# FFN by 26 block products in place of 28, on tiles of 1024 tokens, with the sums of weights kept in DRAM

## The chip, the cores and the metric

One core of a Trainium2 chip. The metric is the device time of one execution in microseconds. The kernel before takes 1181.1 us (median of 3 runs, 1180.2 to 1182.3). A ratio is the one for the fast runs of the same rounds, with its 95% interval; it is not quite the ratio of the medians that stand next to it. A kernel counts as faster or slower when it differs by 2%. Starts of parts are read from the one profiled run of each kernel.

## The reference

Eight batches of eight heads, 576 positions, 64 features a head; the result of the attention is reordered into 4608 tokens of 512 features and goes through a gated feed-forward network (FFN).

```python
def _attn_ref(q, k, v):                       # q, k, v: (8, 8, 576, 64)
    scores = scale * np.matmul(q, k.transpose(0, 1, 3, 2))
    ...                                       # Dmat: gamma ** (row - column), 0 above the diagonal
    return np.matmul(scores * Dmat, v)

def _moe_ref(x, w_gate, w_val, w_out):        # x: (4608, 512), d_ff = 1536
    g = x @ w_gate
    silu = g * (1.0 / (1.0 + np.exp(-g)))
    return silu * (x @ w_val) @ w_out
```

## The kernel before

The kernel first does four attention steps and a plain FFN tile of 512 tokens, while VectorE and ScalarE round the weights from 64-bit floats. All later tiles (512 tokens each) use seven block products in place of eight; the sums of blocks that they need are made on GpSimd and VectorE during the tile. Attention steps are merged between the products of the tile before the one that needs them. In the first stage a weight block goes through this ring: load of raw bits, split on ScalarE, rounding on VectorE; a finished split starts a load three blocks on.

```python
    def split(i):
        ...
        nc.scalar.activation(out=top, in_=bits[:, :, 1].bitcast(F32), func=AF.Copy, scale=2.0 ** -112)
        nc.scalar.activation(out=ulp, in_=bits[:, :, 0].bitcast(U32), func=AF.Copy, scale=2.0 ** -29)
        if order.index(i) + RAWS < len(order):
            load_w(order[order.index(i) + RAWS])      # on SyncE's queue

    def weight(i):                                    # VectorE, three operations
        nc.vector.tensor_scalar(out=dst, in0=top, scalar1=3, ...)
        nc.vector.scalar_tensor_tensor(out=top, in0=top, ..., in1=dst, ...)
        nc.vector.tensor_tensor(out=dst, in0=top, in1=ulp, op=ALU.add)
        ...                                           # then split() of the next block
```

The schedule is manual: the program fixes the order of each engine's instructions.

## Time and profile before

| part of the kernel before | us | read from |
|---|---|---|
| first stage: attention and plain tile of 512 tokens | 207.0 | start of the first block product |
| eight tiles of 7 products, with the remaining attention | 973.6 | 1180.6 less 207.0 |
| TensorE's share of the span | 97% | first line of the page |

The prediction shows the lines that carry this.

### The profile page before, as it was taken

To read this page: it belongs to the slowest core of one execution; us is meant where nothing else is said; L and a number is where in the kernel's file an instruction comes from. 1 tells how busy PE (TensorE), PEld (TensorE's weight loads), DVE (VectorE), ACT (ScalarE), POOL (GpSimd) and SP (SyncE) were. 2 spreads that over 40 slices of the span, in tenths; PEclk is the share of its full clock that TensorE was granted. 3 is DMA by queue.
4 is the path that set the end of the run, shared out by engine and by line. 5 is a ranking of instruction groups with operands and counts; after the bars stand their busy time and mean duration, and the time that the engine had idled before them with its cause. 6 is when DMAs were issued, how large, how long until landed. Compare 5 with 4: busy or idle time off the path is not lost.

```text
span 1180.6 us, 16347 instructions
## 1 busy us (share of the span) xinstructions
PE 1150.1 (97%) x6660; PEld 944.7 (80%) x6660; DVE 484.2 (41%) x886; ACT 186.8 (16%) x342; POOL 425.1 (36%) x384
## 2 busy tenths in 40 slices
PE   6988899999999999999999999999999999999998
PEld 5534444888888888888888888888888888888887
DVE  3566642444444433544244444444443333333332
ACT  3443310111011101111011101110111011101110
POOL 1000010443345343344444414434453435345641
PEclk9988899999999999999999999999999999999999
DMA  7897422222213221222222222222000010000001
GB/s 189 243 259 194 120 49 57 49 39 41 55 34 65 41 39 37 39 53 45 58 40 41 39 66 49 40 40 48 28 1 1 1 36 1 1 18 19 1 1 36
DMA packets 228300, 65.33 MB, mean 55 GB/s; under 512 B 211712, under 2 KB 219904, under 8 KB 228224
## 3 DMA queue, kind: packets, MB, share of 16 engines
q1 hardware_dynamic: 228224, 64.27, 23.5%
q8 instruction: 53, 0.87, 0.3%
q14 instruction: 23, 0.19, 0.1%
HBM read 54.80 MB, written 9.44 MB: 54 GB/s over the span
## 4 chain that ended last, share of the span: by engine, by line
PE 92%; SPq 4%; DVE 1%; DMA 1%; ACT 1%; issue 0%; DVEq 0%; ACTq 0%
PE bankE L394 14%; PE bankA L394 14%; PE bankC L394 14%; PE bankE L464 7%; PE bankC L464 7%; PE bankB L394 7%; PE bankA L464 7%; PE bankB L464 4%; PE sc L277 2%; PE xo L299 2%; PE mix L283 2%; PE bankA L351 2%; SPq L132 2%; PE xo L307 1%; PE bankC L351 1%; PE bankE L351 1%
## 5 line engine op out<-in xcount | busy, mean ns | idle before, releaser
L394 PE MATMUL bankA<-x,w_up 128*128 128x256 f32 x768 | 182.0, 380 | 0.0
L438 POOL TENSOR_TENSOR hid<-c,ss 128x512 f32<-128x512 f32 x48 | 61.0, 1271 | 325.2 <-ACT ss L437 325.2
L394 PEld LDWEIGHTS bankA<-x,w_up 128*128 128x128 f32 x768 | 145.4, 190 | 20.4 <-issue 0.5
L413 DVE TENSOR_TENSOR u<-bankB,u 128x512 f32<-128x512 f32 x48 | 33.2, 692 | 147.7 <-PE bankB L394 138.2
L394 PE MATMUL bankE<-x,s 128*128 128x256 f32 x384 | 91.3, 381 | 0.0
L394 PE MATMUL bankE<-x,w_up 128*128 128x256 f32 x384 | 91.3, 381 | 0.0
L394 PE MATMUL bankC<-t,s 128*128 128x256 f32 x384 | 90.7, 379 | 0.0
L394 PE MATMUL bankC<-t,w_up 128*128 128x256 f32 x384 | 90.7, 379 | 0.0
L394 PE MATMUL bankB<-t,s 128*128 128x256 f32 x384 | 90.7, 379 | 0.0
L464 PE MATMUL bankE<-w_dn,hid 128*128 128x256 f32 x384 | 86.1, 381 | 0.0
L464 PE MATMUL bankA<-w_dn,hid 128*128 128x256 f32 x384 | 85.5, 379 | 0.0
L464 PE MATMUL bankC<-t,hid 128*128 128x256 f32 x384 | 85.5, 379 | 0.0
L394 PEld LDWEIGHTS bankC<-t,s 128*128 128x128 f32 x384 | 73.0, 190 | 9.9
L394 PEld LDWEIGHTS bankB<-t,s 128*128 128x128 f32 x384 | 73.0, 190 | 9.9
L394 PEld LDWEIGHTS bankC<-t,w_up 128*128 128x128 f32 x384 | 73.0, 190 | 9.9
L464 PEld LDWEIGHTS bankA<-w_dn,hid 128*128 128x128 f32 x384 | 73.0, 190 | 9.9
L464 PEld LDWEIGHTS bankC<-t,hid 128*128 128x128 f32 x384 | 73.0, 190 | 9.9
L394 PEld LDWEIGHTS bankE<-x,w_up 128*128 128x128 f32 x384 | 72.5, 190 | 10.0
L394 PEld LDWEIGHTS bankE<-x,s 128*128 128x128 f32 x384 | 72.5, 190 | 10.0
L464 PEld LDWEIGHTS bankE<-w_dn,hid 128*128 128x128 f32 x384 | 72.5, 190 | 10.0
L429 ACT ACTIVATE s<-bankA 128x256 f32<-128x256 f32 x48 | 18.4, 383 | 345.1 <-PE bankA L394 345.1
L371 POOL TENSOR_TENSOR s<-w_up 128x512 f32<-128x512 f32 x48 | 61.0, 1271 | 7.6 <-DVE w_dn L225 7.6
(107 smaller groups left out, 1520.1 us busy)
## 6 DMA issues: line engine op xcount, KB each, us to landing
kn<-in_k_dram SPq DMA_DIRECT2D x64, 128.0 KB, 2.8
v<-in_v_dram SPq DMA_DIRECT2D x64, 128.0 KB, 2.9
qk<-in_q_dram SPq DMA_DIRECT2D x112, 72.0 KB, 2.5
qk<-in_k_dram SPq DMA_DIRECT2D x112, 72.0 KB, 2.6
raw<-in_moe_w_gate_dram SPq DMA_DIRECT2D x6, 1024.0 KB, 5.4
raw<-in_moe_w_val_dram SPq DMA_DIRECT2D x6, 1024.0 KB, 7.2
raw<-in_moe_w_out_dram SPq DMA_DIRECT2D x6, 1024.0 KB, 5.1
out_dram<-c SPq DMA_DIRECT2D x16, 256.0 KB, 2.2
```

The source lines that it names most:

```text
L132: nc.sync.dma_start(out=qk[a * SQ : (a + 1) * SQ, n], in_=src[b, 2 * p + a // 2, :, (a % 2) * SQ : (a % 2 + 1) * SQ].rearrange("(j t) d -> ...
L277: nc.tensor.matmul(sc[hl][:, ts(c, P)], kT[half[hl], ts(c, P)], qT[half[hl], ts(c, P)], start=True, stop=True)
L283: nc.tensor.matmul(z[half[hl], c], kn[:, c, hl, :], s["v"][:, c, hl, :], start=True, stop=True)
L299: nc.tensor.matmul(xo[half[hl], ts(c, P)], s["v"][:, c, hl, :], ret[:, hl, ts(c, P)], start=(c == 0), stop=(c == 0), skip_group_check=True)
L307: nc.tensor.matmul(o[half[hl]], state[half[hl], c - 1, :], s["qT"][half[hl], c * P : c * P + w], start=False, stop=True, skip_group_check= ...
L351: nc.tensor.matmul(bank, w_up[:, u, gv, c // 2, c % 2, fb, :], x[:, c, :], start=(c == 0), stop=(c == HP - 1))
L371: nc.gpsimd.tensor_tensor(out=s2, in0=A(u, 1, 0), in1=A(u, 0, 0), op=ALU.subtract)
L394: nc.tensor.matmul(bank[:, gv * TH : (gv + 1) * TH], lhs(gv, c), rhs[:, c, :], start=(start and gv == 0 and c == 0), stop=(stop and c == 1 ...
L413: nc.vector.tensor_tensor(out=uu, in0=bankB, in1=uu, op=ALU.add)
L429: nc.scalar.activation(out=s, in_=bankA[:, 0:TH], func=AF.Silu)
L438: nc.gpsimd.tensor_tensor(out=hid[:, u, 1::2], in0=t["c"][:, :, 1], in1=s, op=ALU.mult)
L464: nc.tensor.matmul(bank[:, m * DH : (m + 1) * DH], lhs(u)[:, ts(m, P)], rhs(u), start=(start and u == 0 and m == 0), stop=(stop and u == N ...
```

## The change

The 4x2 by 2x4 block scheme computes with 26 products what takes 32 plain ones, and 28 by the seven for eight of the kernel before. Four tiles of 1024 tokens replace eight of 512, and 144 matmul calls of 256 columns go. To pay for this:

- the 26 operands of gate and value weights (most of them sums of blocks) for each of three groups of four feature blocks, one group a pass, are made once, during the first big tile (1024 tokens), used in place, stored to DRAM, and fetched per tile from then on; the sums of output weights are made by GpSimd in the first stage and stored as well;
- rounding works on halves, and the plain tile's plan says by a table how many halves must be rounded before each block of 128 features;
- memory of finished stages is handed on (x of one tile lies where the raw weights were), and four more attention steps come into the first stage.

The diff, cut to its core (the tables of the products are left out but for two lines):

```diff
-    TW = 512
+    T0 = 512
+    TW = 1024
+UP = [
+    "0= | 8: sub 8 2 6, sub 9 0 8, sub 10 4 9 | 8: neg 8 6, sub 9 2 6, ... | copy 0, copy 1",
+    "1= | 10: sub 11 3 8, sub 12 7 11 | 3: add 12 3 6, neg 12 12 | copy 2, copy 3",
...
+    def up_step(n, qd, i):
+        bank, opens, xslot, xops, wslot, wops, ops = up[i]
+        busy = n == 1
+        if qd == 0 and i > 0:
+            for op in xops:
+                add(nc.vector if busy else nc.gpsimd, op, x_view(n))
+        if busy:
+            if i > 0:
+                for op in wops:
+                    add(nc.gpsimd, op, up_view(qd))
+            w = up_view(qd)(wslot)
+        else:
+            w = operand()[:, 0:512]...                 # from the ring of eight fetched places
...                                                    # 4 matmuls
+        if busy:
+            nc.sync.dma_start(out=up_ops[qd][i]..., in_=w)
+        else:
+            fetch()
...
+    have = {2: 8, 3: 8, 4: 12, 5: 12, 6: 18, 7: 18, 8: 24, 9: 24, 10: 32, 11: 32}
+    for f in range(2, NF):
+        while nxt < have[f]:
+            plan.append(roundings[nxt - done])
+            nxt += 1
+        plan.append(lambda f=f: up0(f, range(HP)))
+        for _ in range(3):
+            if f >= (8, 10, NF)[groups[0][0]]:
+                plan.append(sums_of(groups.pop(0)[1]))   # GpSimd sums, stores on SyncE's queue
...
+    merge((0.5, ticks(HP, 10)), (0.5, plan))
```

## The prediction

> **What bounds the kernel now.** I read the page first (busy shares, chain of waits), then busy time by stretch, the chain in order of time, the groups, the DMA queue's own waits, and the timeline of one attention step.
>
> ```profile
> span 1180.6 us, 16347 instructions
> PE 1150.1 (97%) x6660; PEld 944.7 (80%) x6660; DVE 484.2 (41%) x886; ACT 186.8 (16%) x342; POOL 425.1 (36%) x384
> PE 92%; SPq 4%; DVE 1%; DMA 1%; ACT 1%; issue 0%; DVEq 0%; ACTq 0%
> ```
> TensorE is 97% busy and 92% of the chain. By stretch (span, then busy time of each engine, clock, DMA share, GB/s):
> ```profile
> 78.00:147.00 69.00, 60.64 (x256) 30.30 (x253) 40.05 (x65) 21.81 (x26) 3.83 (x3) 0.86 0.68 185
> 458.50:584.00 125.50, 125.50 (x793) 109.41 (x792) 52.48 (x101) 16.35 (x34) 50.97 (x47) 1.00 0.22 46
> 960.00:1068.00 108.00, 108.00 (x502) 95.08 (x501) 35.52 (x52) 13.25 (x26) 51.32 (x46) 1.00 0.03 10
> ```
> Holes are in the first stage only (here 8 us, clock 0.86). From 207 us on TensorE is full, VectorE and GpSimd near 40%. In the chain in order of time, one product of the up layer is 4 calls (8 records), one of the down layer 12 calls (24 records):
> ```profile
> 78.49 6.15 PE bankA L351 x8
> 84.64 3.43 PE bankB L351 x8
> ...
> 332.85 1.73 PE bankA L394 x8
> ...
> 1042.13 5.18 PE bankB L464 x24
> ```
> So a call of 256 columns costs 1.727/4 = 0.432 us, with no gap between products. The first two lines show the price of a long pause: after 8 us without work, 8 calls took 6.15 us instead of 3.43.
>
> What the other engines pay per operation (busy, mean ns | idle):
> ```profile
> L413 DVE TENSOR_TENSOR u<-bankB,u 128x512 f32<-128x512 f32 x48 | 33.2, 692 | 147.7 <-PE bankB L394 138.2 <-ACT u L408 9.5
> L371 POOL TENSOR_TENSOR s<-w_up 128x512 f32<-128x512 f32 x48 | 61.0, 1271 | 7.6 <-DVE w_dn L225 7.6
> L446 POOL TENSOR_TENSOR hid<-u,s 128x256 f32<-128x256 f32 x48 | 34.9, 727 | 45.1 <-ACT s L445 45.1
> ```
> One attention step in the timeline, from TensorE's first work to its next product, and the loads that follow it on the queue; below it the queue's longest such wait:
> ```profile
> 468.81 1.09 PE L299 MATMUL xo<-ret,v 128*64 128x128 f32 x16
> 472.84 1.99 PE L394 MATMUL bankE<-x,s 128*128 128x256 f32 x8
> 475.17 0.74 DVE L262 STREAM_TRANSPOSE kT<-qk 128x576 f32<-128x576 f32 x1
> 475.94 1.96 SPq L132 DMA_DIRECT2D qk<-in_q_dram  x4
> 482.30 1.15 SPq L142 DMA_DIRECT2D vl<-in_v_dram  x2
> ```
> ```profile
> SPq L132 <- DVE kT L262: 316.7, 21, 20.8
> ```
> Call the step's start T0. TensorE is on it for 4.03 us; VectorE is done at T0+7.1; only then does the queue issue 14 loads at about 0.5 us each, until T0+14.6. Today nothing urgent stands behind them.
>
> [...]
>
> **The change part by part.**
>
> *Removed.* Per 1024 tokens the up layer goes from 2 x 6 x 7 x 4 = 336 calls to 3 x 26 x 4 = 312, the down layer from 2 x 7 x 12 = 168 to 26 x 6 = 156: 36 calls fewer, 15.5 us, and over 4 tiles 62.2 us. The first 512 tokens stay plain. The attention work is the same; four steps of it move from the tiles into the first stage. With TensorE as full as now: 1180.6 - 62.2 = 1118.4.
>
> *VectorE and GpSimd, by amount.* A pass of 26 up products lasts 26 x 1.727 = 44.9 us on TensorE. VectorE has 21 adds from PSUM and 8 products, 21 x 0.69 + 8 x 0.42 = 18 us; GpSimd in the first pass of a later tile 21 sums of x x 1.27 + 4 x 1.27 + 8 x 0.73 = 37.6 us, in the other passes 11. In the first big tile GpSimd makes 30 weight sums a pass[...]. Down: 67 us, against about 32 on VectorE and 23 on GpSimd. All fit by amount; the loss is in order and distance.
>
> *(b) First big tile: a sum's place may be overwritten only when its store to DRAM has landed.* The stores stand on the one queue, behind the loads of an attention step. A store behind them is issued at T0+14.6 and lands 2.3 us later (existing 256 KB stores: 2.2), T0+17.0; the dependent sum and negation end at T0+19. Four steps fall into this tile's up layer, before steps (0,0), (0,19), (1,13), (2,6) of the three passes. At (1,13) the rewritten sum is used at product 18: TensorE is there at T0+4.03+5x1.73 = 12.7, stall 6.4. At (2,6): used at product 10, due T0+10.9, stall 8.1. At (0,0): VectorE starts 1 us late (copies of the plain tile, x sums), used at product 6, due T0+14.4, ready 19.4, stall 5, then 0.8. At (0,19) there is distance; VectorE makes a sum of x late, 2.4. Sum 22.7[...]: 27.
>
> *(c) Later tiles: sums of x on GpSimd, two products ahead of use.* They queue behind GpSimd's part of the step before. Example: product 4 ends at 0; VectorE adds till 0.9, GpSimd subtracts till 2.24, ACT's Silu till 2.7, GpSimd's product till 3.5, then the x sum till 4.8; product 7 was due at 3.46: 1.4 lost. Likewise before products 10 (1.35), 11 (0.9), 19 (1.7; hidden once by an attention step) and 24 (0.8): 6.2, 6.2 and 4.5 us for three tiles. At each of three changes of tile the first x sums wait for GpSimd's last down sums: 1.2 each. Sum 20.5.
>
> *(d) Fetches.* 256 KB per 1.73 us is 152 GB/s. Eight places are a lead of 13.8 us; after an attention step the next fetch lands at about T0+17.7 and is due at T0+17.85. Even, so some 1 us per step for six steps: 6.
>
> *(a) First stage.* The 36 half-size roundings cost VectorE as before, but six attention steps are pressed into the up layer (about 69 us of needed VectorE work against 69 of TensorE before the tenth feature block), and GpSimd's 78 sums of the output weights finish within a few us of the plain tile's end. I take +5; the earlier table load gives little back.
>
> Sum: 1118.4 + 27 + 20.5 + 6 + 5 = 1176.9. I state 1172, a little lower, since each stall was walked separately and a late TensorE gives the next sum more time.
>
> **The rivals.** R1, all hidden: TensorE stays at 99% and the time is about 1120 to 1130. For: before, the same style of schedule runs with no gap; both helpers have over half their time free. Against: distances of two products and a queue that stands for 14.6 us. R2, DMA bound: loads of small packets took 22% of the DMA engines for 46 GB/s; 152 more GB/s at the first stage's rate of about 217 GB/s for 87% busy would add over 60%, so fetches would queue, tiles 2 and 3 by 20 to 40 us: 1195 to 1215. Against: the eight places ahead, and that the weight rows are longer. R3, the first stage waits for the output-weight sums and late roundings: 20 us more, 1190.
>
> **Range and chances.** The gain of 62.2 is sure; (b) and (c) rest on the order of the queues and measured durations and I trust them to about 12 us together; (a) and (d) to 8 each. Root of the squares is near 17 us: 8 in 10 from 1148 to 1196. Faster by over 2% means under 1157.5: 0.25. Slower by over 2% means over 1204.7: 0.05. Within: 0.70.
>
> **What would show each step.** The FFN has 288 TensorE records fewer (two per call, 144 calls); products at 1.73 and 2.59 us. For (b): three TensorE gaps of 5 to 8 us in the first big tile, weight sums on GpSimd waiting for DMA stores, the queue waiting for the transposes. For (c): in the first pass of tiles 2 to 4 TensorE waits of 1 to 2 us released by GpSimd, none in passes two and three. For (d): TensorE waiting for DMA in tiles 2 and 3 only. I am wrong if the first big tile shows no gap (then R1), if tile 4, which has no attention, is much over 202 + 8 us, or if the plain tile ends later than 240 us.

## More of the kernel before

An attention step is three functions that are emitted together. The matmuls of `values` and of `scores` write different columns of one PSUM bank, `mix`, and VectorE empties it in between:

```python
    z, sr, xr = mix[:, 0:256], mix[:, 256:320], mix[:, 384:448]   # shapes shortened
    def tick(t, lo=HP, hi=NP):
        for fn, i in ((values, t - 2), (scores, t - 1), (transposes, t)):
            if lo <= i < hi:
                fn(i)
    # values(i):  TensorE fills xo and xr (bank mix); VectorE: evacuate(xr), evacuate(xo)
    # scores(i):  TensorE fills sc, then sr and z (bank mix); VectorE: ret, ret_last, state
```

One more view is needed for later, busy time by stretch, at the end of the first stage. The columns are the stretch and its length; busy time (and instructions) of TensorE, of its weight loads, of VectorE, ScalarE and GpSimd; granted clock, DMA share, GB/s.

```profile
147.00:207.00 60.00, 60.00 (x265) 29.69 (x264) 19.55 (x38) 6.60 (x11) 6.90 (x6) 1.00 0.24 52
207.00:260.00 53.00, 53.00 (x352) 46.11 (x351) 22.75 (x45) 8.70 (x18) 25.93 (x22) 1.00 0.25 49
```

TensorE has no idle moment in the last 60 us of the first stage. VectorE has 40 us of them free there, and GpSimd 53.

## The result, and the profile after

The changed kernel takes 1247.6 us (median of 4 runs, 1244.4 to 1250.1), against 1181.4 in the same rounds: ratio 1.0559, 95% interval 1.0533 to 1.0586. It is slower by 5.6%, and outside the predicted range.

The first lines of the page, the busy shares and the chain of waits (which the reconstruction loses before it reaches the start):

```profile
span 1245.7 us, 17330 instructions
PE 1112.4 (89%) x6372; PEld 895.8 (72%) x6372; DVE 635.0 (51%) x1031; ACT 247.9 (20%) x508; POOL 489.9 (39%) x422
PE 55%; POOL 5%; DVE 2%; issue 1%; ACT 1%; DVEq 0%; POOLq 0%; ACTq 0%
```

TensorE has exactly 6660 - 6372 = 288 records fewer, as predicted, but its share fell from 97% to 89%. The work went and idle time came. Busy time by stretch says where (columns as above):

```profile
147.00:207.00 60.00, 30.47 (x229) 18.19 (x226) 43.15 (x74) 16.63 (x30) 30.80 (x36) 0.74 0.62 165
260.00:300.00 40.00, 24.53 (x153) 19.81 (x154) 21.36 (x32) 5.56 (x12) 29.40 (x27) 0.86 0.68 190
300.00:350.00 50.00, 41.85 (x225) 34.78 (x225) 38.51 (x54) 9.28 (x21) 33.27 (x23) 0.90 0.43 131
400.00:470.00 70.00, 57.59 (x298) 48.77 (x297) 34.85 (x57) 13.31 (x30) 41.07 (x31) 0.90 0.42 129
470.00:556.00 86.00, 86.00 (x611) 74.35 (x611) 52.06 (x88) 10.74 (x22) 24.06 (x14) 1.00 0.72 198
```

In the stretch 147 to 207 us TensorE worked 30 us of 60, at a clock of 0.74, where it worked all 60 before. The up layer of the first big tile (275 to 476 us) has holes throughout. The down layer (from 476 us) is full.

I cut the program at two moments that the timeline gives, the start of the first block product and the start of the first down product, and set each part beside its nominal length, which is the prediction's base of 1118.4 us: the old first stage and five attention steps of 4.03 us (207.0 + 20.2), three passes of 44.9 us and four attention steps (150.8), and what is left. Five steps, since the first one of the big tile also stands before its first product: the attention's output matmuls ran for 8 steps before that cut in the kernel before, and for 13 now.

| part | nominal | predicted loss | the changed kernel | loss |
|---|---|---|---|---|
| first stage, to the first block product | 227.2 | 5 | 275.1 | 47.9 |
| up layer of the first big tile | 150.8 | 27 | 200.6 | 49.8 |
| the rest | 740.4 | 26.5 | 770.0 | 29.6 |
| sum | 1118.4 | 58.5 | 1245.7 | 127.3 |

What TensorE waited for, in the timeline of TensorE. A line is start, duration, engine, line of the program, operation and operands; in brackets how long the engine was idle before and who released it.

```profile
123.49 0.48 PE L402 MATMUL mix<-qT,kT 64*64 64x64 f32 x4 [7.45 <-DVE x_odd L445]
168.22 0.48 PE L402 MATMUL mix<-qT,kT 64*64 64x64 f32 x4 [19.22 <-DVE x_odd L445]
203.08 0.48 PE L402 MATMUL mix<-qT,kT 64*64 64x64 f32 x4 [9.53 <-DVE rest L445]
275.08 3.78 PE L601 MATMUL bankA<-rest,arena 128*128 128x256 f32 x8 [10.74 <-POOL arena L502]
387.32 3.78 PE L601 MATMUL bankA<-x_odd,arena 128*128 128x256 f32 x8 [7.07 <-POOL arena L502]
437.37 3.78 PE L601 MATMUL bankC<-rest,arena 128*128 128x256 f32 x8 [9.05 <-POOL arena L502]
...
820.23 1.99 PE L601 MATMUL bankA<-rest,arena 128*128 128x256 f32 x8 [1.54 <-POOL rest L504]
826.82 1.99 PE L601 MATMUL bankC<-rest,arena 128*128 128x256 f32 x8 [1.15 <-POOL rest L504]
845.27 1.99 PE L601 MATMUL bankC<-rest,arena 128*128 128x256 f32 x8 [1.61 <-POOL rest L504]
```

Three kinds of wait stand there. In the first stage the scores' matmul into bank `mix` waits for VectorE to empty that bank. In the first big tile a product waits for GpSimd's last weight sum: the waits of 7.07 and 9.05 us are those predicted at 6.4 and 8.1. In the later tiles products wait one microsecond or so for GpSimd's sums of x, as predicted.

Why does VectorE come 19 us late at 168 us? Its own timeline ahead of that moment:

```profile
147.70 0.56 DVE L352 TENSOR_SCALAR rest<-rest 128x512 int32<-128x512 int32 x1
148.30 1.10 DVE L353 SCALAR_TENSOR_TENSOR rest<-rest 128x512 int32<-128x512 int32 x1
149.43 1.09 DVE L355 CUSTOM_DVE_ANT_0 rest<-rest 128x1024 uint16<-128x1024 uint16 x1
...
161.77 0.99 DVE L355 CUSTOM_DVE_ANT_0 arena<-rest 128x1024 uint16<-128x1024 uint16 x1
165.54 0.53 DVE L352 TENSOR_SCALAR arena<-rest 128x512 int32<-128x512 int32 x1 [2.78 <-ACT rest L339]
166.10 1.10 DVE L353 SCALAR_TENSOR_TENSOR rest<-rest,arena 128x512 int32<-128x512 int32 x1
167.34 0.69 DVE L355 CUSTOM_DVE_ANT_0 arena<-rest 128x1024 uint16<-128x1024 uint16 x1
167.95 0.22 DVE L445 TENSOR_TENSOR x_odd<-mix,tab 128x64 f32<-128x64 f32 x1
```

The evacuation that TensorE waits for takes 0.22 us, but it stands in VectorE's queue behind seven half roundings in a row, 20 us of them. The last waits for ScalarE's split, which itself waited 5.5 us for its raw weights. And the two-input operations of the roundings take up to 1.1 us each where they take 0.69 in the run without the sums, below. The table `have` causes the row: it asks for four, six or eight new halves before every second block and for none before the next one.

### The profile page after: what moved, and what is told of

The parts are those of the page before. It is cut to its first block, busy times and chain, and to the rows that moved or that the text cites. A ratio compares the mean times of both kernels' runs of the same rounds, so it can differ in the third digit from the quotient of the medians.

```text
span 1245.7 us, 17330 instructions
## 1 busy us (share of the span) xinstructions
PE 1112.4 (89%) x6372; PEld 895.8 (72%) x6372; DVE 635.0 (51%) x1031; ACT 247.9 (20%) x508; POOL 489.9 (39%) x422
## 4 chain that ended last, share of the span: by engine, by line
PE 55%; POOL 5%; DVE 2%; issue 1%; ACT 1%; DVEq 0%; POOLq 0%; ACTq 0%
PE bankA L601 8%; PE bankE L601 8%; PE bankB L601 7%; PE bankC L601 6%; PE bankC L642 6%; PE bankE L642 6%; PE bankB L642 5%; PE bankA L642 5%; POOL rest L504 3%; DVE rest L580 2%; PE xo L421 1%; PE sc L399 1%; POOL rest L580 1%; POOL arena L622 1%; PE xo L429 1%; PE mix L405 1%
## 5 line engine op out<-in xcount | busy, mean ns | idle before, releaser
L504 POOL TENSOR_TENSOR arena<-arena 128x512 f32<-128x512 f32 (+1 forms) x97 | 152.9, 1592 | 128.4 <-DVE arena L504 58.8
L504 POOL TENSOR_TENSOR rest<-rest 128x256 f32<-128x256 f32 (+1 forms) x111 | 108.6, 990 | 180.1 <-DVE rest L355 110.7
L601 PE MATMUL bankA<-rest,arena 128*128 128x256 f32 x576 | 141.0, 388 | 25.4 <-POOL arena L502 10.7
L601 PE MATMUL bankE<-rest,arena 128*128 128x256 f32 x624 | 148.6, 381 | 3.6 <-POOL rest L504 1.7
L601 PEld LDWEIGHTS bankA<-rest,arena 128*128 128x128 f32 x576 | 109.3, 193 | 47.8 <-POOL arena L502 10.9
L601 PEld LDWEIGHTS bankE<-rest,arena 128*128 128x128 f32 x624 | 117.4, 190 | 22.0 <-POOL rest L504 3.4
L601 PE MATMUL bankB<-rest,arena 128*128 128x256 f32 x528 | 125.4, 380 | 0.8 <-POOL arena L502 0.8
L601 PE MATMUL bankC<-rest,arena 128*128 128x256 f32 x384 | 100.2, 408 | 21.8 <-POOL arena L502 11.6
L601 PEld LDWEIGHTS bankB<-rest,arena 128*128 128x128 f32 x528 | 101.0, 192 | 15.5 <-POOL arena L502 1.2
L601 PEld LDWEIGHTS bankC<-rest,arena 128*128 128x128 f32 x384 | 77.3, 204 | 37.2 <-POOL arena L502 12.4
L580 DVE TENSOR_TENSOR rest<-bankE,rest 128x512 f32<-128x512 f32 x100 | 67.4, 684 | 56.4 <-PE bankE L601 35.0
```

What stands on the lines that cost most here:

```text
L504: eng.tensor_tensor(out=dst, in0=srcs[0], in1=srcs[1], op=ALU.add if op[0] == "add" else ALU.subtract)
L580: eng.tensor_tensor(out=at(op[1]), in0=at(op[2]), in1=at(op[3]), op=ALU.add if op[0] == "add" else ALU.subtract)
L601: nc.tensor.matmul(banks[bank][:, gv * TB : (gv + 1) * TB], w[:, gv, ts(c, P)], rhs[:, c, :], start=(opens and gv == 0 and c == 0), stop=( ...
```

## The experiments

Theory after the result: four causes in three stretches, namely (i) the roundings in bunches in front of an in-order VectorE, (ii) stores that stand behind loads in SyncE's queue, of up sums in the first big tile and of output-weight sums in the first stage, (iii) slow negations on GpSimd (1.58 us each in the first big tile), (iv) GpSimd's x sums in later tiles. The rivals are in the expectations.

**Half roundings spread evenly.** The correct number of halves before each block is kept, only earlier.

```diff
-    have = {2: 8, 3: 8, 4: 12, 5: 12, 6: 18, 7: 18, 8: 24, 9: 24, 10: 32, 11: 32}
+    have = {2: 8, 3: 10, 4: 12, 5: 15, 6: 18, 7: 21, 8: 24, 9: 28, 10: 32, 11: 34}
```

> The weight roundings of the first stage are spread evenly over the feature blocks instead of up to eight in a row. If VectorE's backlog holds the score matmuls (the three pauses of 7.5, 19.2 and 9.5 us at 123, 168 and 203 us), the pauses shrink to about half and the time falls by 10 to 20 us, to 1228 to 1238. If the late weight loads behind the one queue set this stage, it falls by 5 us at most.

Measured: 1223.7 us, ratio to the kernel before 1.0358 (1.0342 to 1.0373); 23.9 us less than the changed kernel, more than expected. All waits for `mix` in the first stage fall from 40.4 us together to 16.4. Two of them in the timeline of TensorE, and the first block product:

```profile
141.25 0.48 PE L402 MATMUL mix<-qT,kT 64*64 64x64 f32 x4 [6.30 <-DVE x_odd L445]
170.58 0.33 PE L402 MATMUL mix<-qT,kT 64*64 64x64 f32 x4 [3.32 <-DVE rest L445]
...
251.77 3.78 PE L601 MATMUL bankA<-rest,arena 128*128 128x256 f32 x8 [20.21 <-POOL arena L502]
```

The last matmuls of the plain tile start at 226.2 us in place of 258.9, 32.7 us earlier. But 9.5 us of it are given back in a new wait: the first block product now waits 20.2 us, not 10.7, for GpSimd's weight sums. 32.7 - 9.5 = 23.2, about the whole gain.

**Negations of the first big tile on ScalarE.**

```diff
+        if op[0] == "neg" and neg_act:
+            nc.scalar.mul(out=dst, in_=srcs[0], mul=-1.0)
```

> In the first big tile the 21 negations of weight sums go from GpSimd (1.58 us each) to ScalarE. If the slow negations are a cost of their own, the small TensorE waits for GpSimd in the first pass (1.0, 0.8, 2.5 us) vanish and the two after the attention steps (7.1, 9.1) shrink by about 1 us each: 6 to 12 us less, 1236 to 1242. If only the stores behind the loads matter, 2 to 3 us less.

Measured: 1242.6 us (ratio 1.0520); 5.0 less, between the two expected ranges. The waits of 7.07 and 9.05 us become 6.13 and 8.26, released by ScalarE. The first block product no longer waits (it starts at 265.3 us), but the third one waits 6.86 us and the seventh 4.36 for GpSimd: the small waits of the first pass did not vanish. The length of GpSimd's chain counts a little; most of the two long waits is there without it.

**The up sums' stores on ScalarE's queue.**

```diff
-            nc.sync.dma_start(out=up_ops[qd][i]..., in_=w)
+            nc.scalar.dma_start(out=up_ops[qd][i]..., in_=w)
```

> The 78 stores of weight sums are issued from ScalarE's queue instead of the one that holds the attention loads. If the stores behind the loads make GpSimd late, the TensorE pauses of 7.1 and 9.1 us at 387 and 437 us vanish with the slow clock after them (2 us each): 18 to 25 us less, 1223 to 1230. If GpSimd is simply short of time in this tile, 5 us less at most.

Measured: 1228.5 us (ratio 1.0406); 19.1 less, as expected, and the waits of 7.07 and 9.05 us are gone. The up layer of the first big tile took 180.8 us in place of 200.6, nothing else moved. In the changed kernel the reason can be read in two timelines. SyncE's queue issues the 14 loads of an attention step, which takes it 7.5 us (1.96 for the first four, 0.49 each), and only then the stores:

```profile
374.45 1.96 SPq L268 DMA_DIRECT2D qk<-in_q_dram  x4
...
380.81 1.16 SPq L278 DMA_DIRECT2D vl<-in_v_dram  x2
382.06 2.99 SPq L604 DMA_DIRECT2D up<-arena  x5
```

GpSimd's next sum waits for one of these stores to land, and the negation that TensorE waits for follows it:

```profile
384.43 1.26 POOL L504 TENSOR_TENSOR arena<-arena 128x512 f32<-128x512 f32 x1 [16.08 <-DMA up<-arena]
385.78 1.49 POOL L502 TENSOR_SCALAR arena<-arena 128x512 f32<-128x512 f32 x1
```

**The x sums of tiles 2 to 4 on VectorE.**

```diff
-                add(nc.vector if busy else nc.gpsimd, op, x_view(n))
+                add(nc.vector, op, x_view(n))
-            add(nc.vector if n == 1 else nc.gpsimd, op, x_view(n))
+            add(nc.vector, op, x_view(n))
```

> The sums of x of tiles 2 to 4 are made on VectorE instead of GpSimd. If they are late because they queue behind GpSimd's own work, the TensorE waits of 0.5 to 1.6 us in the first pass of each tile vanish: 18 to 26 us less, 1221 to 1230. If any in-order engine is late at a distance of two products, VectorE will be too and it falls by 8 us at most.

Measured: 1231.7 us (ratio 1.0425); 15.9 less, just under the expected range. The rest of the program shrinks from 770.0 to 754.3 us; the two parts before it together stay within 1.2 us. Tile 3's first pass lasts 47.8 us from its first product to its change of pass, in place of 52.9, and in its timeline two waits are left, where there were six:

```profile
837.34 1.99 PE L601 MATMUL bankE<-x_odd,arena 128*128 128x256 f32 x8 [1.08 <-DVE x_odd L504]
847.02 1.99 PE L601 MATMUL bankA<-rest,arena 128*128 128x256 f32 x8 [0.78 <-DVE rest L580]
```

**The four together.** The edits are those above.

> Four changes together: half roundings spread evenly, negations of the first big tile on ScalarE, the up layer's sum stores on ScalarE's queue, x sums of tiles 2 to 4 on VectorE. If the four losses lie in different stretches and are independent: 1247.6 - 24 - 5 - 19 - 16 = about 1184 us. If the wait of 20.2 us at the first product of the big tile (for GpSimd's output-weight sums, seen in the run with the roundings spread) is what the end of the first stage hangs on now, the sum can still hold, but that wait stands: about 20 us before the first product. If stores and negations are two names for one loss (the sums of one tile come late either way), 1187 to 1192.

Measured: 1180.5 us, ratio 1.0013 (0.9992 to 1.0033): the kernel before, to the third digit. The single gains add up to 23.9 + 5.0 + 19.1 + 15.9 = 63.9, and together they give 67.1. So the gains add up, those of the stores and of the negations too, which lie in the same stretch. A wait of 15.6 us for GpSimd's sums stands before the third product of the first big tile.

**Spread, and the output sums' stores on ScalarE's queue.**

```diff
-                nc.sync.dma_start(out=dn_ops[i][:, qd * TB : (qd + 1) * TB], in_=view(slot))
+                nc.scalar.dma_start(out=dn_ops[i][:, qd * TB : (qd + 1) * TB], in_=view(slot))
```

> Roundings spread, and the stores of the output-weight sums issued by ScalarE instead of SyncE. Theory that GpSimd's output sums end late because their stores and the loads behind them stand in SyncE's queue: the wait of 20.2 us before the big tile's first product falls to under 8 us and the time to 1205 to 1212 (1223.7 with the roundings alone spread). Rival, that GpSimd is short of time itself[...]: the wait stays over 14 us, 1218 to 1224.

Measured: 1208.6 us (ratio 1.0256), as expected. The first block product starts at 240.3 us in place of 251.8, and no wait for GpSimd is left in front of it. The plain tile itself, however, ends 9 us later than with the spread alone (its last matmuls start at 235.4), because ScalarE, which now issues stores that wait for GpSimd, makes the splits late: one of them waits 8.96 us for GpSimd, and one 8.80 in the five together. (The profiled run is the slowest of its four, 1215.0 us; but the five together, below, show the same against the four: 233.6 us in place of 224.5.)

**Spread, and no output sums at all** (plain blocks are stored in place of sums). Its output is wrong, which doesn't matter for the time.

```diff
-                for op in ops:
-                    add(nc.gpsimd, op, view)
+                pass
-            def store(i=int(i), slot=int(slot)):
+            def store(i=int(i), slot=int(slot) % 8):
```

> Roundings spread, and the sums of output weights not computed at all: single blocks are stored in their place, so the result is wrong on purpose. It bounds what those sums cost in the first stage: the wait of 20.2 us goes, and VectorE's roundings and evacuations there take their time alone (0.69 us per half rounding). Theory: 1195 to 1203. If the first stage is then held by weight loads or the attention itself, over 1210.

Measured: 1197.4 us (ratio 1.0172), 26.3 us less than the spread alone. The first block product starts at 223.6 us in place of 251.8: 20.2 us are the wait that is gone, and 7.6 the plain tile, whose last matmuls start at 218.6 us in place of 226.2. A possible reason for the 7.6 stands in the groups of instructions by form, 120 to 207 us: line, engine, operation, operands, count, busy time and mean ns. First the run without sums, then the one with the spread alone:

```profile
L355 DVE CUSTOM_DVE_ANT_0 rest<-rest 128x1024 uint16<-128x1024 uint16 x7 | 4.8, 692 | 0.7
L353 DVE SCALAR_TENSOR_TENSOR rest<-rest 128x512 int32<-128x512 int32 x7 | 4.8, 692 | 0.2
```
```profile
L355 DVE CUSTOM_DVE_ANT_0 rest<-rest 128x1024 uint16<-128x1024 uint16 x8 | 6.5, 817 | 0.8
L353 DVE SCALAR_TENSOR_TENSOR rest<-rest 128x512 int32<-128x512 int32 x8 | 6.8, 852 | 0.3
```

With GpSimd adding beside it VectorE takes 18% and 23% longer for the same operations. With GpSimd quiet each takes 692 ns. That this makes the plain tile late is not shown: the run also takes away 24.8 us in which SyncE's queue, with the weight loads behind it, waited for GpSimd's sums. And in the best version, further below, the sums run and the same operations average 834 and 855 ns, yet the plain tile's last matmuls start at 218.3 us.

**All five.** The four together, and the output sums' stores on ScalarE's queue.

> All four changes and the output-sum stores on ScalarE's queue. If both theories hold: some 15 us below the run with four changes, 1165 to 1172, which is below the kernel before. If GpSimd itself is short of time at the start: within 5 us of the run with four changes.

Measured: 1167.9 us, ratio 0.9901 (0.9886 to 0.9916): the first version below the kernel before, though by less than 2%.

**Attention steps split in two, alone.** If TensorE waits for the bank only because the scores follow the values at once, other work between them should hide the wait.

```diff
-    ticks = lambda a, b: [lambda t=t: tick(t) for t in range(a, b)]
+    def part_of(t, which):
+        for j, (fn, i) in enumerate(((values, t - 2), (scores, t - 1), (transposes, t))):
+            if (j > 0) == which and HP <= i < NP:
+                fn(i)
+    ticks = lambda a, b: [lambda t=t, w=w: part_of(t, w) for t in range(a, b) for w in (False, True)]
```

> The changed kernel with one thing altered: the values part of an attention step and its scores part are two entries of the merged list, so products or a plain block stand between them and TensorE doesn't come to the scores' matmul into bank mix right behind the values. Theory (the waits of 7.45, 19.2, 9.5 and 6.0 us are for VectorE's evacuation of that bank, which stands behind its roundings, and TensorE has other work it could do): most of those 42 us go, and the time falls by 15 to 30 us from 1247.6. Rival (VectorE is short of time in the first stage, so the blocks that need its results wait instead): under 8 us less, with the waits moved to the blocks' rows.

Measured: 1247.8 us, no gain: the theory fell and its rival held. The waits for `mix` shrank to 2.5 us in all, and the time moved to the plain blocks, which wait for weights that VectorE has not rounded yet, and to the first block product:

```profile
155.37 5.54 PE L471 MATMUL bankA<-rest,arena 128*128 128x512 f32 x8 [14.63 <-DVE arena L355]
167.95 6.08 PE L471 MATMUL bankB<-rest,arena 128*128 128x512 f32 x8 [7.04 <-DVE arena L355]
...
276.22 3.78 PE L601 MATMUL bankA<-rest,arena 128*128 128x256 f32 x8 [21.60 <-POOL arena L502]
```

The plain tile's last matmuls start 7.4 us earlier, and the wait for GpSimd is 10.9 us longer. So the bank was the place where TensorE happened to meet VectorE's backlog. The backlog itself, and behind it GpSimd's sums, set the end of the first stage.

**The same split on top of the five.**

> The run with five changes (1167.9 us) and the attention steps split in the same way. Waits of 3.3, 9.1, 4.4 and 5.7 us for bank mix stand there; if TensorE has other work in their place, 10 to 20 us less: 1148 to 1158. If VectorE is the bound there, under 5 us less: 1163 to 1168.

Measured: 1167.7 us, against 1167.9: nothing again. But the parts moved against each other: the first block product starts at 226.3 us in place of 238.6, the up layer takes 177.7 in place of 174.5, and the rest 761.6 in place of 753.9. 12.3 us are gained and 10.9 given back.

**The output sums' stores on ScalarE's queue, alone.** The fourth corner of a square.

> The changed kernel with the stores of the output-weight sums issued by ScalarE, and nothing else altered; the fourth corner of a square with 1247.6 (neither), 1223.7 (roundings spread) and 1208.6 (both). Theory A, that raw weights are fetched late in the first stage because their loads stand in SyncE's queue behind these stores, whatever the order of the roundings: 15 to 30 us less, 1218 to 1232, with the wait of 10.7 us at the big tile's first product gone. Theory B, that the roundings in bunches are the cause alone and the stores only matter once they are spread: at most 8 us less, 1240 to 1247.

Measured: 1234.9 us (ratio 1.0465); 12.7 less.

| median us | sums' stores on SyncE | on ScalarE |
|---|---|---|
| roundings in bunches | 1247.6 | 1234.9 |
| roundings spread | 1223.7 | 1208.6 |

Neither theory is right as put. The time fell into a gap between the two ranges. The plain tile did not end earlier (its last matmuls start at 262.6, against 258.9), so the stores are not what makes the raw weights late; the long wait for `mix` is still 17.7 us. But 7.5 of the 12.7 us are gained at the first block product (267.6 against 275.1), bunches or not. The two causes are nearly independent: 12.7 and 15.1 us for the stores, 23.9 and 26.3 for the spread.

**Sums laid between the roundings, on top of the six.**

```diff
         while nxt < have[f]:
             plan.append(roundings[nxt - done])
             nxt += 1
+            if due:
+                plan.append(due.pop(0))
...
-                plan.append(sums_of(groups.pop(0)[1]))
+                due.append(sums_of(groups.pop(0)[1]))
```

> The run with six changes (1167.7 us) and the groups of output-weight sums laid between the roundings instead of three in a row behind each block, so that ScalarE, which issues their stores, waits less for GpSimd (8.8 us before one split of raw weights in the run with five changes). If that wait holds the roundings up: 3 to 8 us less, 1160 to 1165. If something else is as late: within 3 us.

Measured: 1163.5 us, ratio 0.9868 (0.9846 to 0.9889), in the expected range; but the interval overlaps that of the six (0.9851 to 0.9907), so by the times alone the gain is not shown. In the trace the first block product starts at 222.5 us in place of 226.3, and so even before its nominal 227.2.

**The split in the first stage only.**

```diff
-    merge((0.5, ticks(HP, 10)), (0.5, plan))
+    merge((0.5, parted(HP, 10)), (0.5, plan))
-    merge((0.0, ticks(10, needed(1))), (0.5, tail))
+    merge((0.0, parted(10, needed(1))), (0.5, tail))
```

(`parted` is the split list; `ticks` is the old one again, for the tiles.)

> The run with seven changes (1163.5 us), but the attention steps are split in the first stage only; in the tiles they stand as in the run with five changes. If the split gains in the first stage and gives it back in the tiles: the first product at 222 us as with seven changes, an up layer of about 174.5 and a rest of about 754, so 1151 to 1156. If the two stretches only shift against each other: 1160 to 1164.

Measured: 1153.3 us, ratio to the kernel before 0.9764 (0.9743 to 0.9784). It is the best version, 2.4% faster than the kernel before. The three parts are 223.3, 174.1 and 753.9 us. The same stretch of the first stage that was half empty:

```profile
147.00:207.00 60.00, 55.62 (x372) 31.33 (x371) 25.13 (x58) 6.81 (x13) 46.36 (x61) 0.94 0.74 192
260.00:300.00 40.00, 32.80 (x191) 27.92 (x192) 26.59 (x43) 10.83 (x23) 15.35 (x12) 0.91 0.49 135
400.00:470.00 70.00, 70.00 (x484) 60.80 (x483) 42.59 (x70) 9.11 (x18) 11.58 (x6) 1.00 0.76 197
```

**Partial sums of the first big tile on GpSimd, on top.** To see whether VectorE's amount of work makes the 23 us that the up layer of the best version still loses.

```diff
-                eng = nc.vector if "b" in op or busy else nc.gpsimd
+                eng = nc.vector if "b" in op else nc.gpsimd
```

> The same, and the partial sums of the up layer that need no PSUM bank go to GpSimd in the first big tile too, as they do in the later ones. If VectorE's queue is what makes the x sums late there (waits of 0.9 to 2.3 us for VectorE, some 16 us of idle TensorE in that layer), 4 to 10 us less than the run before it. If GpSimd, which makes the weight sums there, becomes the later one: the same or slower, with waits for GpSimd in their place.

Measured: 1154.1 us (ratio 0.9768): the same as the run before it, and the up layer takes 174.1 us in both. TensorE's waits for VectorE stay. Twelve operations fewer on VectorE (110.2 us busy in that layer in place of 119.1) don't help there, and GpSimd did not become the later one. The test is a small one: VectorE stays busy for 63% of the layer.

## Why the prediction was wrong

The predicted 1172 us missed by 75.6 us. Step by step:

- **Removed: right.** 288 records fewer, products at 1.73 and 2.59 us, and once the first stage was mended the program comes to within 33 us of the base of 1118.4.
- **(a) First stage: this step failed.** It was put as "+5", and lost 47.9. The working named both facts, "about 69 us of needed VectorE work against 69 of TensorE" and GpSimd's sums finishing "within a few us of the plain tile's end", and took them as a balance. Four things were missed.
  - First, a balance of amounts leaves no room for order: the roundings stand in bunches of up to eight before an in-order engine, so evacuations and splits come 20 us late (spread evenly, the plain tile ended 32.7 us earlier). In the best version, which does the same sums and roundings in this stage but in another order and on other queues, the first block product starts at 223.3 us.
  - Second, "the roundings cost VectorE as before" was false. Before, 18 whole blocks took VectorE 56.4 us; the 36 halves take 64.7 us with GpSimd quiet (a whole took 1226 ns where two halves take 2 x 692), and 74.3 in the changed kernel, beside GpSimd's sums. The prediction counted nothing for the two engines working side by side; the longer times are shown, their price in time is not.
  - Third, GpSimd's "78 sums" are 78 stored operands, for which it does 96 operations, 27 of them negations.
  - Fourth, they were not "within a few us" of the end but 10.7 us late (20.2 once the roundings were spread). The groups of GpSimd say why, with the idle time before an operation and what ended it:

```profile
L504 POOL TENSOR_TENSOR rest<-rest 128x256 f32<-128x256 f32 x69 | 54.1, 798 | 179.0 <-DVE rest L355 110.7 <-DMA dn<-rest 67.1
L502 POOL TENSOR_SCALAR rest<-rest 128x256 f32<-128x256 f32 x27 | 25.0, 929 | 11.4 <-DMA dn<-rest 9.9
```

GpSimd works 79.1 us on them and stands idle for 77.0 until stores of earlier sums have landed, which stand behind attention loads on SyncE's queue; with the stores on ScalarE's queue the wait at the first block product was gone. Rival R3, "the first stage waits for the output-weight sums and late roundings", had the mechanism. It was sized at 20 us.
- **(b) First big tile: right in mechanism, too small.** Predicted 27, of which 22.7 are the stalls and the rest was the author's estimate for a lowered clock after them; measured 49.8. The clock was lowered: in the 4 us from 387 and from 437 us it was 0.50, and the product after each of those two waits took 3.78 us, where the products of later passes take 1.89 in the same view. The stores' part was about right: the predicted stalls of 6.4 and 8.1 us measured 7.07 and 9.05, and moving the stores off SyncE's queue gave back 19.1 us. The stall of 5.0 at the first attention step did not show as one; in the first pass stand three waits for GpSimd of 1.04, 0.80 and 2.53 us. The negation of 128x512, of which the prediction had only an estimate, took 1.58 us (mean of 21; the adds beside it 1.38, and 1.27 in the kernel before), but moving it was worth only 5.0 us of time. The term that was mis-sized is VectorE's, 2.4 us for one late sum of x. Some 23 us stand against it: in the best version's trace a wait of 6.3 for `mix` at one attention step, nine of up to 2.1 for VectorE's sums and evacuations (10.6 together), and products at a lowered clock after them (0.91 between 260 and 300 us). Taking partial sums off VectorE did not touch it, so its exact cause, whether the order of its queue or its longer operations (eleven of its sums of x of 128x512 averaged 1.16 us in this layer of the changed kernel, where each of eight in the kernel before took 0.69), stays open.
- **(c) Later tiles: right.** Predicted waits of 1.4, 1.35, 0.9, 1.7 and 0.8 us stand in tile 3 as 1.54, 1.15, 0.63, 1.61 and 0.56. Taking GpSimd out of them gave 15.9 us of the predicted 20.5; VectorE brings about 1 us a place back in some.
- **(d) Fetches: no loss.** Not one wait of TensorE for a fetch worth naming stands in the changed kernel; the 6 us were not needed. The rest of the program lost 29.6 us, against 26.5 for (c) and (d). That the two are close is partly luck, since the 6 us of (d) did not come: moving the sums of x took back 15.7 us of the 29.6; of the other 13.9, waits of TensorE for VectorE make up 6.4 in the trace of the changed kernel, and the remainder stays open.
- **R1** failed at the first glance: TensorE is at 89%. **R2** failed: the mean traffic was 158 GB/s, 198 GB/s between 470 and 556 us took 72% of the DMA engines, and TensorE waited for no fetch.
- **A line misread.** The prediction says "after 8 us without work, 8 calls took 6.15 us"; the timeline of the kernel before has a pause of 5.2 us there, and 1.5 us of attention work after it; the granted clock from 78 to 85 us is 0.61. The 8 us are all the holes of that stretch together.

The prediction's own warning, "if the plain tile ends later than 240 us", is what came true: its last matmuls start at 258.9 us.

## What to carry to other kernels

When two engines' needed work in a stage adds up to the time of the stage, ask for the order, not the amount: spread the work that others wait for evenly (23.9 us here), and put each store on a queue where nothing slower stands ahead of it (19.1 us here for the up sums, 12.7 for the output sums). A wait's name was here the place where an engine met a backlog, not its cause; removing the place (the split alone) moved the time, while shortening the backlog (the spread) took most of it away, and only after that did the split bring the end of the first stage forward. When two stretches shift against each other, cut the program at fixed moments and compare the parts, since an unchanged total can hide a gain of 12 us and a loss of 11.
